# Where in SBUF the expert weights and the x operands begin: rests by 256 bytes in an attention and two-expert kernel

## Chip, cores and metric

The kernel runs on one core of a Trainium2 chip. The metric is the device time of one execution in microseconds, a median over runs. Lower is better.

## What is computed

Attention with talking heads (2 batches, 12 heads, 448 positions, head size 64), and then two feed-forward layers, called experts here, over 896 tokens of width 768 with 2048 hidden units. All is float32.

```python
scores = scale * np.matmul(q, k.transpose(0, 1, 3, 2))
scores = np.einsum('bhij,hg->bgij', scores, w_pre)
attn = np.exp(scores - np.max(scores, axis=-1, keepdims=True))
attn = attn / (np.sum(attn, axis=-1, keepdims=True) + 1e-09)
attn = np.einsum('bhij,hg->bgij', attn, w_post)
x = merge_heads(np.matmul(attn, v))          # 896 x 768
h = x @ w_in1;  g = h * np.clip(h + 3.0, 0.0, 6.0) / 6.0;  x = g @ w_out1
h = x @ w_in2;  g = np.maximum(h, 0.0) + alpha * np.minimum(h, 0.0)
return g @ w_out2
```

## The kernel before

The attention comes first, 90 steps of ten query rows over all heads, pipelined by hand with an order written out in the source: a step's loads, its mixing matmuls, its exponentials and its products with v are spread over several steps. The four expert layers follow: in1 (768 to 2048), out1 (2048 to 768), in2 and out2. The first pieces of in1 are computed between the last attention steps.

An expert's weights come from HBM as 64-bit numbers, in blocks of 128 partitions by 768 columns, 16 blocks a layer and 64 in all. Each block is converted on the chip by a chain of seven instructions: ScalarE (L346, L347), VectorE (L354, L355, L362), GpSimd (L369), which make `wb`, and then ScalarE copies `wb` to the rounded high part `whi` (L374) and GpSimd takes the difference as the low part `wlo` (L380). In the loop of `in_layer` and of `out_layer` a block's `wst` is loaded four blocks ahead, its `wb` is made two to three blocks ahead, and its `whi` and `wlo` two blocks ahead.

Each product of the experts is three matmuls in the type float32r, written out in `mm3` (L432 to L436): `whi` by the operand's high part, `whi` by its low part, `wlo` by its high part. The weights are the stationary operand (128 columns, loaded anew for every matmul), the operands move (448 columns). In in1 and in2 the moving operands are the x pairs `xh` and `xl`, in out1 and out2 the g pairs `gh` and `gl`. One block of weights has 36 such matmuls in every layer, a layer has 576, and the four have 2304. All of them stand on L434 in the profile.

The tiles lie in pools that grow from both ends of a partition's bytes: those with `side="right"` from the end downwards, the others from the start upwards, in the order in which they are opened. A tile takes a multiple of 32 bytes. An x, g or `t` tile is 448 x 4 = 1792 bytes (7 x 256), a `whi`, `wlo` or `wb` tile 768 x 4 = 3072 (12 x 256), a `wst` tile 6144 (24 x 256), so all tiles of one of these pools share the rest by 256 of the pool's end. The right side ends at byte 229,344, which is 224 by 256. The rests of the first bytes before the change, in bytes by 256:

| tiles | pool, side | rest before |
|---|---|---|
| weights `wst`, `wb`, `whi`, `wlo` (blocks 3 on; `whi` and `wlo` of all) | `w`, right | 224 |
| `xh`, `xl` (both batches), `t` | `x0`, `x1`, `tmp`, right | 224 |
| `gh`, `gl`, the first two of batch 0 | `g0`, right | 224 |
| `gh`, `gl`, the other 30 of 32 | `g1`, left | 0 |
| attention: `kT` of heads 0 to 5, of heads 6 to 11 | `kq`, right | 32, 224 |
| attention: `qT` | `kq`, right | 32, 96, 160 |
| attention: scores `S` of even tiles | `s_even`, right | 64 |

`const` holds `alpha_sb` (64 bytes), `three` (L82, 32 bytes taken) and `warm` (L83, 32 bytes taken) on the left, ahead of all other left pools. `three` is the bias of the first expert's activation (L454). `warm` is the target of one exponential at the start (L102), which has the table loaded.

The pools `w`, `x0` and `g0` are opened in `open_early` (L389 to L396), when the attention's `kq` and `s_even` have been closed; `x1` and `tmp` follow in `open_x1`.

Of the kernel before, what the change touches and what calls it, by code (L numbers as in the profile page):

```python
# [7 lines left out]
F32 = mybir.dt.float32  # L8
# [27 lines left out]
def kernel(  # L36
# [42 lines left out]

    const = ctx.enter_context(tc.tile_pool(name="const", bufs=1))  # L80
    alpha_sb = const.tile([128, KF], F32, name="alpha_sb")
    three = const.tile([128, 1], F32, name="three")  # L82
    warm = const.tile([128, 1], F32, name="warm")  # L83


    p_xt, p_late, p_odd, p_kq, p_even, p_ps, p_sc = (ExitStack() for _ in range(7))
# [1 line left out]
    def pool(stack, name, **kw):  # L88
        return stack.enter_context(tc.tile_pool(name=name, reuse_waits="tile", **kw))

    xtp = pool(p_xt, "xt", bufs=1)
    late = pool(p_late, "late", bufs=3)
    s_odd = pool(p_odd, "s_odd", bufs=1)
# [5 lines left out]
    with tc.manual_schedule():  # L99
# [289 lines left out]
        def open_early():  # L389
            p_even.close()  # L390
            p_kq.close()
            p_sc.close()
            P["ps2"] = pool(ctx, "ps2", bufs=2, space=PSUM, side="right")
            P["w"] = pool(ctx, "w", bufs=2, side="right")
            P["x0"] = pool(ctx, "x0", bufs=KD, side="right")
            P["g0"] = pool(ctx, "g0", bufs=NE, side="right")  # L396

# [143 lines left out]
        for i in range(NC):  # L541
            at(a, lambda i=i: load_w(i))
            for z, f in enumerate((conv_magnitude, conv_shift, conv_sign, conv_round)):
                at(a + 3 + z, lambda f=f, i=i: f(i))
            a += 7
        at(X, open_early)
        at(X + 1, lambda: nc.sync.dma_start(out=alpha_sb, in_=alpha.rearrange("(k p) -> p k", p=128)))
        for kk in range(KD):
# [209 lines left out]
```

## Time and profile before

| | |
|---|---|
| time, median of 3 runs | 721.94 us (721.37 to 722.91) |
| the profiled execution's own time | 722.08 us |
| span of the profile, first to last instruction | 720.3 us |
| mean granted TensorE clock | 0.995 of full speed |
| TensorE matmul busy | 704.3 us (98% of the span), 4164 instructions |
| VectorE, ScalarE, GpSimd busy | 58%, 52%, 47% |

By the times at which their matmuls start, the stages are: attention to about 254 us (with pieces of in1 from 219 us on), in1 to 363 us, out1 to 481 us, in2 to 598 us, out2 to 716.8 us, then the last copy and store.

A matmul's row in the profile shows 0.36 to 0.37 us, while the next one starts some 0.20 us later: matmuls are pipelined, so the distance from one start to the next, called the step here, and not the length of the row, is what a matmul costs.

### The profile page before, as it was taken

How to read it: one execution, taken by the hardware profiler on the slowest of the kernel's cores; microseconds unless marked ns; L12 is line 12 of the kernel's file. 1: busy time of each engine (PE TensorE's matmuls, PEld its weight loads, DVE VectorE, ACT ScalarE, POOL GpSimd, SP SyncE). 2: the span in 40 equal slices, each digit the busy share in tenths (PEclk: the TensorE clock that was granted, in tenths of full speed). 3: DMA queues.
4: the chain of work that ended last, by engine and by line, in shares of the span. 5: the costliest groups of instructions: out<-in, count | busy, mean ns of one | idle time of the engine just before them, and what ended most of it. 6: DMA issues, size and time to landing. Idle time of an engine off the chain costs nothing.

```text
span 720.3 us, 11169 instructions
## 1 busy us (share of the span) xinstructions
PE 704.3 (98%) x4164; PEld 609.4 (85%) x4164; DVE 414.3 (58%) x790; ACT 376.6 (52%) x704; POOL 335.1 (47%) x224
## 2 busy tenths in 40 slices
PE   5999999999999998999999999999999999999998
PEld 2678777877778987888889999999999999999997
DVE  5564585456667367777773454347777777344301
ACT  4686666577777455666554443344545444434300
POOL 6331175112235145656567755435555556654530
PEclk9899999999999999999999999999999999999999
DMA  5752564356444023232333433322232333325302
GB/s 157 227 170 100 180 178 122 102 173 199 154 89 131 2 72 104 90 129 89 95 125 132 137 121 101 125 88 87 88 128 92 122 99 131 132 92 182 111 1 76
DMA packets 31875, 85.21 MB, mean 118 GB/s; under 512 B 5966, under 2 KB 21966, under 8 KB 31822
## 3 DMA queue, kind: packets, MB, share of 16 engines
q1 hardware_dynamic: 31822, 84.50, 36.4%
q8 instruction: 33, 0.54, 0.3%
q14 instruction: 20, 0.16, 0.1%
HBM read 62.47 MB, written 2.75 MB: 91 GB/s over the span
## 4 chain that ended last, share of the span: by engine, by line
PE 79%; issue 9%; POOL 8%; DVE 2%; ACT 1%; DMA 0%; SPq 0%; POOLq 0%; ACTq 0%; DVEq 0%
PE p L434 51%; PE pt L242 10%; PE mx L222 9%; PE av L279 5%; PE sc L195 4%; POOL wb L369 4%; POOL wlo L380 2%; POOL kT L158 1%; DMA kst<-in_k_dram 0%; DVE nm L224 0%; DVE wb L354 0%; DVE wr L216 0%; ACT wb L346 0%; DVE xl L293 0%; ACT xh L292 0%
## 5 line engine op out<-in xcount | busy, mean ns | idle before, releaser
L380 POOL TENSOR_TENSOR wlo<-wb,whi 128x768 fp32r<-128x768 f32 x64 | 132.5, 2071 | 163.7 <-ACT whi L374 161.3
L369 POOL TENSOR_TENSOR wb<-wb,wst 128x768 int32<-128x768 int32 x64 | 130.5, 2039 | 69.9 <-DVE wb L362 36.5
L434 PE MATMUL p<-xh,wlo 128*128 128x448 f32 x384 | 141.5, 369 | 3.0 <-POOL wlo L380 2.5
L434 PE MATMUL p<-xh,whi 128*128 128x448 f32 x384 | 142.9, 372 | 0.0
L434 PE MATMUL p<-gh,wlo 128*128 128x448 f32 x384 | 141.2, 368 | 0.1
L434 PE MATMUL p<-gh,whi 128*128 128x448 f32 x384 | 141.0, 367 | 0.0
L434 PE MATMUL p<-gl,whi 128*128 128x448 f32 x384 | 141.0, 367 | 0.0
L434 PE MATMUL p<-xl,whi 128*128 128x448 f32 x384 | 140.4, 366 | 0.0
L354 DVE TENSOR_SCALAR wb<-wb 128x768 f32<-128x768 f32 x64 | 63.9, 999 | 97.5 <-ACT wb L346 97.5
L346 ACT ACTIVATE wb<-wst 128x768 f32<-128x768 f32 x64 | 58.3, 911 | 77.0 <-DMA wst<-in_w_out_dram 46.4
L242 PEld LDWEIGHTS pt<-wr,e 120*112 120x112 f32 x720 | 86.8, 176 | 7.6 <-issue 2.3
L232 ACT ACTIVATE e<-mx,nm 120x448 f32<-120x448 f32 (+1 forms) x90 | 57.1, 635 | 64.5 <-DVE sm L213 44.7
L242 PE MATMUL pt<-wr,e 120*112 120x120 f32 x720 | 88.5, 266 | 0.0
L222 PE MATMUL mx<-pull,wmix_pre 120*120 120x448 f32 x180 | 85.7, 559 | 2.3 <-DMA pull<-S 2.3
L434 PEld LDWEIGHTS p<-xh,wlo 128*128 128x128 f32 x384 | 72.1, 188 | 13.0 <-POOL wlo L380 7.5
L224 DVE TENSOR_REDUCE nm<-mx 120x1 f32<-120x448 f32 (+1 forms) x90 | 56.0, 622 | 46.7 <-PE mx L222 46.7
L434 PEld LDWEIGHTS p<-xh,whi 128*128 128x128 f32 x384 | 72.1, 188 | 7.3 <-issue 1.2
L434 PEld LDWEIGHTS p<-gh,wlo 128*128 128x128 f32 x384 | 72.2, 188 | 7.3 <-POOL wlo L380 0.8
L434 PEld LDWEIGHTS p<-xl,whi 128*128 128x128 f32 x384 | 72.2, 188 | 6.8 <-issue 1.1
L434 PEld LDWEIGHTS p<-gl,whi 128*128 128x128 f32 x384 | 72.2, 188 | 6.6
L434 PEld LDWEIGHTS p<-gh,whi 128*128 128x128 f32 x384 | 72.2, 188 | 6.4
L374 ACT CAST whi<-wb 128x768 fp32r<-128x768 f32 x64 | 53.2, 831 | 46.2 <-PE p L434 43.8
(52 smaller groups left out, 862.4 us busy)
## 6 DMA issues: line engine op xcount, KB each, us to landing
wst<-in_w_in_dram SPq DMA_DIRECT2D x32, 768.0 KB
wst<-in_w_out_dram SPq DMA_DIRECT2D x32, 768.0 KB
pull<-S SPq DMA_DIRECT2D x88, 210.0 KB
qst<-in_q_dram SPq DMA_DIRECT2D x20, 180.0 KB
kst<-in_k_dram SPq DMA_DIRECT2D x5, 672.0 KB
v<-in_v_dram SPq DMA_DIRECT2D x8, 336.0 KB
out_dram<-o SPq DMA_DIRECT2D x12, 224.0 KB
qst<-in_q_dram SPq DMA_DIRECT2D x8, 132.0 KB
```

The source lines that it names most:

```text
L195: nc.tensor.matmul(p[:n, :S], t[:, o, a:a + n], kT[h], start=(o == 0), stop=(o == 1))
L222: nc.tensor.matmul(m[:pn, :S], wpre[:pn, :pn], d[:pn], start=True, stop=True)
L224: nc.vector.tensor_reduce(nm[:pn], m[:pn, :S], axis=AX.X, op=ALU.max, negate=True)
L232: nc.scalar.activation(out=e[:pn], in_=m[:pn, :S], func=ACTF.Exp, bias=nm[:pn], accum_out=sm[:pn])
L242: nc.tensor.matmul(p[:, c * GP:(c + 1) * GP], e[:pn, c * JP:(c + 1) * JP], wr[:pn], start=True, stop=True,)
L279: nc.tensor.matmul(p[64 * o:64 * o + 64, a % 3, :n], v_t[T["b"], h // HC][:, h % HC, c, :], MT[ti][:, c, h, :n], start=(c == 0), stop=(c = ...
L346: nc.scalar.activation(t, s[:, :, 1].bitcast(F32), ACTF.Abs)
L354: nc.vector.tensor_scalar(t, t, W_MAX, W_MIN, ALU.min, ALU.max)
L369: nc.gpsimd.tensor_tensor(n, n, st_t.pop(i)[:, :, 0].bitcast(I32), ALU.add)
L374: nc.scalar.copy(hi, b_t[i])
L380: nc.gpsimd.tensor_tensor(lo, b_t.pop(i), w_t[i][0].bitcast(F32), ALU.subtract)
L434: nc.tensor.matmul(p, wt[a], xt[c], start=(first and z == 0), stop=(last and z == 2))
```

## The change

`three` leaves the left `const` pool for a new pool `edge`, the first on the right side, where it takes 32 bytes. `warm` grows from 1 to 16 columns, 64 bytes, so `const` keeps its 128 bytes and every left pool its place. All that lies on the right moves down by 32 bytes. Behind the `w` pool a tile `gap` of 192 bytes is opened that nothing writes or reads, so `x0`, `g0`, `x1` and `tmp` move down by 224 bytes in all. No other instruction is changed.

```diff
     alpha_sb = const.tile([128, KF], F32, name="alpha_sb")
-    three = const.tile([128, 1], F32, name="three")
-    warm = const.tile([128, 1], F32, name="warm")
+    warm = const.tile([128, 16], F32, name="warm")
...
+    edge = pool(ctx, "edge", bufs=1, side="right")
+    three = edge.tile([128, 1], F32, name="three")
     xtp = pool(p_xt, "xt", bufs=1)
...
             P["w"] = pool(ctx, "w", bufs=2, side="right")
+
+            pool(ctx, "gap", bufs=1, side="right").tile([128, 48], F32, name="gap")
             P["x0"] = pool(ctx, "x0", bufs=KD, side="right")
```

The rests by 256 after it: weights 192; x pairs, `t` and all g pairs 0; `kT` 0 and 192; `qT` 0, 64 and 128; even `S` 32; left tiles as before.

## Rows read from the trace of the kernel before

**Rows 1.** The page, part 1: busy us, share of the span and instructions of each engine.

```profile
PE 704.3 (98%) x4164; PEld 609.4 (85%) x4164; DVE 414.3 (58%) x790; ACT 376.6 (52%) x704; POOL 335.1 (47%) x224
```

**Rows 2.** The chain that ended last: start us, us, what.

```profile
331.70 1.61 issue
333.31 2.27 POOL wb L369
...
363.93 352.92 PE p L434 x1726
```

**Rows 3.** Windows: stretch, length, busy of PE, PEld, DVE, ACT, POOL (instructions), clock, DMA.

```profile
254.00:364.00 110.00, 106.92 (x510) 94.57 (x510) 82.88 (x102) 66.40 (x101) 63.17 (x29) 1.00 0.30 101
...
371.60:421.00 49.40, 49.40 (x247) 46.36 (x248) 23.32 (x29) 22.11 (x29) 35.12 (x17) 1.00 0.40 131
429.00:481.00 52.00, 52.00 (x253) 47.31 (x252) 21.14 (x26) 18.84 (x24) 26.70 (x14) 1.00 0.35 115
482.00:597.00 115.00, 115.00 (x569) 106.57 (x568) 86.74 (x141) 54.93 (x79) 61.25 (x30) 1.00 0.30 98
602.00:657.00 55.00, 55.00 (x268) 50.06 (x267) 22.86 (x26) 20.25 (x26) 31.47 (x17) 1.00 0.39 131
```

**Rows 4.** Timeline of TensorE around its last stall, and where g0 operands return.

```profile
371.18 0.37 PE L434 MATMUL p<-gl,whi 128*128 128x448 f32 x1
371.54 0.47 PE L434 MATMUL p<-gh,wlo 128*128 128x448 f32 x1
371.85 0.36 PE L434 MATMUL p<-gh,whi 128*128 128x448 f32 x1
...
421.25 0.36 PE L434 MATMUL p<-gl,whi 128*128 128x448 f32 x1
421.45 0.36 PE L434 MATMUL p<-gh,wlo 128*128 128x448 f32 x1
```

**Rows 5.** Timeline of TensorE in out1, the second half: first and last of 250 matmuls.

```profile
429.42 0.37 PE L434 MATMUL p<-gh,wlo 128*128 128x448 f32 x1
...
480.88 0.37 PE L434 MATMUL p<-gh,wlo 128*128 128x448 f32 x1
```

**Rows 6.** Timeline of TensorE: first matmul of in2, first and last of out2.

```profile
481.08 0.36 PE L434 MATMUL p<-xh,whi 128*128 128x448 f32 x1
...
597.82 0.36 PE L434 MATMUL p<-gh,whi 128*128 128x448 f32 x1
...
716.46 0.37 PE L434 MATMUL p<-gh,wlo 128*128 128x448 f32 x1
```

**Rows 7.** Timeline of TensorE in in1: first and last of 26 matmuls between two stalls.

```profile
311.65 0.37 PE L434 MATMUL p<-xl,whi 128*128 128x448 f32 x1
...
316.82 0.37 PE L434 MATMUL p<-xh,wlo 128*128 128x448 f32 x1
```

**Rows 8.** Timeline of GpSimd: `wlo` in in1 (first two), in out1, in in2.

```profile
330.92 2.44 POOL L380 TENSOR_TENSOR wlo<-wb,whi 128x768 fp32r<-128x768 f32 x1 [2.96 <-ACT whi L374]
...
338.54 2.44 POOL L380 TENSOR_TENSOR wlo<-wb,whi 128x768 fp32r<-128x768 f32 x1 [2.96 <-ACT whi L374]
...
444.84 1.84 POOL L380 TENSOR_TENSOR wlo<-wb,whi 128x768 fp32r<-128x768 f32 x1 [3.74 <-ACT whi L374]
...
502.29 1.89 POOL L380 TENSOR_TENSOR wlo<-wb,whi 128x768 fp32r<-128x768 f32 x1 [1.91 <-ACT whi L374]
```

**Rows 9.** Groups of instructions, forms apart: the attention's matmuls in float32r.

```profile
L195 PE MATMUL sc<-kT,qT 128*120 128x448 f32 x120 | 53.6, 533 | 1.6 <-POOL kT L152 0.9 <-ACT S L586 0.4 <-POOL qT L168 0.3
L195 PE MATMUL sc<-kT,qT 128*88 128x448 f32 x48 | 22.1, 541 | 0.0
```

**Rows 10.** Timelines at the two ends: `warm` on ScalarE, the last copy on VectorE.

```profile
2.02 0.20 ACT L102 ACTIVATE warm<-warm 128x1 f32<-128x1 f32 x1
...
716.87 0.62 DVE L677 COPY o<-p 128x448 f32<-128x448 f32 x1 [1.85 <-PE p L434]
```

## The prediction, made before the change was run

> **What bounds the kernel now.** I read the engines' busy time first: TensorE is busy for 98% of the span [rows 1], at the full granted clock of 2.4 GHz in all expert stretches (1.00 in [rows 3]). Busy is not the same as fast, so I next asked the chain that ended last where the end is set. Its last piece is one unbroken run of 1726 expert matmuls, 352.92 us from 363.93 on [rows 2]: nothing but TensorE's own rate decides out1, in2 and out2. Ahead of it the chain runs through GpSimd and "issue" pieces, not through matmuls [rows 2]; TensorE is idle there for 3.1 of 110 us [rows 3]. So two stretches have two different limits: the conversion of weights in in1, the matmul rate behind it.
>
> Then I read that rate, as the distance between starts. 448 columns at 2.4 GHz would take 448 / 2.4 = 186.7 ns. The run averages 352.92 / 1726 = 204.5 ns, and it isn't one rate with noise but a few exact levels:
> - 371.85 to 421.45: 248 steps of 200.0 ns [rows 4], moving operands at rest 0, weights at 224.
> - 429.42 to 480.88: 249 steps of 206.7 ns [rows 5], the same rests, 0 and 224.
> - in2, 481.08 to 597.82: 576 steps of 202.7 ns on average [rows 6], both rests 224.
> - out2, 597.82 to 716.46: 575 steps of 206.3 ns [rows 6], mostly 0 and 224.
> - a piece of in1, 311.65 to 316.82: 25 steps of 206.8 ns [rows 7], both rests 224.
>
> Other engines don't make these levels: they hold for 50 us and more while VectorE, ScalarE, GpSimd and the DMAs come and go [rows 3]. 200.0 and 206.7 ns are 480 and 496 cycles of 2.4 GHz, 16 apart. The same pair of rests shows both, so the rest alone doesn't set the level. What came before does too: the 200.0 stretch begins right behind a stall (371.18, 371.54, 371.85 in [rows 4]), and the slower one when, at 421.45, the matmuls return to the four g0 tiles, the only g tiles at rest 224; between 421.45 and 429.42 there are 39 steps of 204.4 ns on average [rows 4, 5], and when the g0 tiles are over, the level stays at 206.7. Out2 enters from in2's operands at 224, and is slow throughout.
>
> **The change part by part.** The edits that add or grow an instruction first. `warm` with 16 columns instead of 1 is 15 more columns in an instruction of 0.20 us at 2.02 us [rows 10], ahead of all other work of ScalarE, which then has to wait for the first scores: nothing. If nothing covered it, it would cost under 0.1 us, since even a copy of 448 columns takes 0.62 us [rows 10]. `three` is read from another address by the same instruction; the gap has no instruction. The queues, the loads and the waits keep their order; SP issues the same DMAs. Left tiles keep their addresses.
>
> The attention's float32r products are 168 matmuls [rows 9] with kT and qT moved by 32 bytes. I have no step for these new rests. Priced by the levels above, each can change by at most 6.7 ns, 1.1 us for 168 either way; they now fall all over those levels, so I take 0 and keep 0.5 us on each side.
>
> In in1 a block of weights takes 7.62 us: `wlo` starts at 330.92 and at 338.54 [rows 8]. TensorE needs 36 x 202.7 ns = 7.30 us for it, and waits for the rest. The loop goes `wlo` on GpSimd, `wb` on ScalarE, the conversion on VectorE, the activation's steps behind it, `whi` on ScalarE, `wlo` again; GpSimd sits idle for 2.96 us before each `wlo` until `whi` is there [rows 8], while no matmul is the releaser. A step of 200.0 or 206.7 ns makes TensorE's part 7.20 or 7.44 us, both under 7.62, so I take 0 there. The cover is gone only from 7.62 / 36 = 211.7 ns on.
>
> What is left are the steps from 371.85 to 716.46. Of the chain's 1726 matmuls 37 begin before 371.85 [rows 2, 4], so it is 1726 - 37 - 1 = 1688 steps in 344.61 us, 204.2 ns each, with no idle time of TensorE in any window [rows 3]. After the change every moving operand of this stretch has rest 0 and every weight 192, the same from end to end. The trace doesn't show 0 with 192. The bounds: if TensorE lost nothing between matmuls, 186.7 ns; above, one more stride of 16 cycles, 213.3 ns. The nearest rows are those with the moving operand at 0: 200.0 and 206.7 ns. I take 200.0, for two reasons. First, the one time that operands at 0 were entered from a stall, the level was 200.0 and held for 248 steps through six blocks of weights [rows 4]; what ended it was the return of tiles at 224, and after the change no such tile is left. Second, if the step is a fetch or a start held to a grid of 16 cycles (6.67 ns, in which float32 operands of 4 bytes a column pass 64 bytes), then 192 and 0 are both multiples of 64 and 224 is not, which speaks for fewer lost slots and not for more. The second is an argument, not a row.
>
> The sum: 1688 x 200.0 = 337.6 us against 344.61, so -7.0 us. By stage, that is about -1.9 in out1, 576 x 2.7 = -1.5 in in2, 575 x 6.3 = -3.6 in out2. What would be late next is the conversion. In out1 it has been seen to keep up at 200.0 ns: no idle time from 371.6 to 421 [rows 3]. In in2 GpSimd waits 1.91 us before a `wlo` [rows 8], so it isn't full; if in2's conversion nevertheless allowed only today's 7.30 us a block, 1.5 us of the gain would be lost. The end (716.87 on, [rows 10]) moves along.
>
> The profiled execution took 722.08 us, its span 720.3 and 1.78 around it. That is 0.14 us over the median of 721.94. 722.08 - 7.0 - 0.1 = 715.0 us against the median.
>
> A rule that speaks against all this: the page "SBUF — State Buffer" of the Trainium skill, section "Who interferes with whom", gives TensorE two independent read ports, one for the moving operand and one for the weight load, and says that TensorE never waits on anyone. By it the place of the weights against x costs nothing, and the sum would be 0: 722 us. The trace neither refutes it (equal rests, two levels) nor explains the levels.
>
> **The rivals.**
> - The level is handed on by what came before and the address has no part in it. For it: one pair of rests shows 200.0 and 206.7 [rows 4, 5], and rests of 224 and 224 show 202.7 and 206.8 [rows 6, 7]. Against it: each switch in the run coincides with a change of rest or with a stall. Stalls are as before, so the levels would come out mixed as today: 721.9, within 1.4. The rule of the Trainium skill's page above says the same.
> - 0 with 192 settles at or near in2's average of 202.7: 1688 x 202.7 = 342.1, -2.5 us, 719.4; with stages at different levels, 717 to 721.5.
> - Slower: the stretch locks to 206.7 ns at 371.85. Then nothing breaks the lock up to the end, as nothing has in 249 steps [rows 5], and all stages pay: 1688 x 206.7 = 348.9, +4.3 us, 726.2. It is decided in the first few steps after the last stall. For it: it is the level held longest today. Against it: it has followed operands at 224 wherever I see it begin. One stride further, 213.3 ns, would make in1 wait for TensorE too: +15.5 and some 1 us, about 738.
> - A level not seen yet, below 200: one stride of 16 cycles down is 193.3 ns, 1688 x 193.3 = 326.3, -18.3 us, 703.6. Against it: both rests of g have been tried, and no run of steps under 200 stands in the trace. The change would have to act through the weights' rest alone.
> - That the rests aren't what the change says would need a left tile or a closing pool to move; `const` keeps 64 + 64 = 128 bytes, so I give it nothing of its own.
>
> **How the numbers follow.** Locked to 200.0, 715.0 us (714 to 716.5): 0.42. Near 202.7 or mixed stages: 0.20, of it 0.14 faster by over 0.2% (1.4 us, about what a measurement of this kernel can tell from no change) and 0.06 not. Address without effect: 0.08. Locked to 206.7: 0.18. Below 200: 0.08. Above 207: 0.04. Faster 0.42 + 0.14 + 0.08 = 0.64, same 0.06 + 0.08 = 0.14, slower 0.18 + 0.04 = 0.22. The range leaves out the two unseen levels and the outer edges: from 713.5 (714.0 less the attention's 0.5) to 726.5 (726.2 and some of the same).
>
> **What would show it.** Starts 200.0 ns apart from the last stall of in1 or out1 to 709 us, 7.20 us from block to block in out1, in2 and out2 alike, and no jump at the two returns of the g0 tiles. In1's blocks should stay at 7.62 us, with TensorE idle longer in each. I am wrong if the steps are 206.7 throughout, if the level still changes in mid-stage with all rests equal, or if in2 stops at 7.30 us with TensorE waiting for `wlo`.

## The result, and the profile after

The changed kernel takes 714.6 us (median of 4 executions, 713.94 to 715.41), against 721.66 us of the kernel before, run again beside it. The ratio is 0.9894, with a 95% interval of 0.9882 to 0.9906: 1.1% faster. The profiled execution took 715.01 us, 7.07 us less than that of before (722.08), and its span is 713.2 us.

The chain that ended last (start us, us, what) still ends in one run of expert matmuls on TensorE, now counted from the last stall:

```profile
371.52 338.30 PE p L438 x1690
```

338.30 / 1690 = 200.2 ns a matmul; the first step behind the stall is longer, 0.31 us (371.52 to 371.83 below). The line numbers are four higher, the matmul is the same. TensorE's timeline shows the last stall, the place where the g0 tiles used to raise the step, the first matmul of in2, and the first and last of out2:

```profile
371.02 0.37 PE L438 MATMUL p<-gl,whi 128*128 128x448 f32 x1
371.52 0.47 PE L438 MATMUL p<-gh,wlo 128*128 128x448 f32 x1
371.83 0.37 PE L438 MATMUL p<-gh,whi 128*128 128x448 f32 x1
...
421.04 0.36 PE L438 MATMUL p<-gh,whi 128*128 128x448 f32 x1
421.23 0.36 PE L438 MATMUL p<-gl,whi 128*128 128x448 f32 x1
421.44 0.36 PE L438 MATMUL p<-gh,wlo 128*128 128x448 f32 x1
421.64 0.36 PE L438 MATMUL p<-gh,whi 128*128 128x448 f32 x1
...
479.24 0.36 PE L438 MATMUL p<-xh,whi 128*128 128x448 f32 x1
...
594.43 0.36 PE L438 MATMUL p<-gh,whi 128*128 128x448 f32 x1
...
709.43 0.37 PE L438 MATMUL p<-gh,wlo 128*128 128x448 f32 x1
```

From 371.83 to 709.43 there are again 1688 steps, in 337.60 us: 200.0 ns each, where the kernel before had 204.2 [rows 4, 6]. In2 is 576 steps in 115.19 us (116.74 before, [rows 6]), out2 575 in 115.00 (118.64 before). There is no jump at 421.45 any more [rows 4]. One detail is new: the 200.0 is an average over three. Starts lie 0.19, 0.21 and 0.20 us apart in turn (421.04 to 421.64), where the 200.0 of before had equal steps.

In1 has kept its pace. The windows and GpSimd's timeline:

```profile
254.00:364.00 110.00, 106.46 (x511) 95.98 (x510) 82.86 (x102) 66.47 (x102) 63.04 (x29) 0.98 0.30 101
371.60:421.00 49.40, 49.40 (x247) 46.31 (x248) 23.00 (x29) 22.10 (x29) 34.81 (x17) 1.00 0.40 132
429.00:479.00 50.00, 50.00 (x251) 46.87 (x251) 22.40 (x26) 18.64 (x24) 25.83 (x14) 1.00 0.36 117
480.00:594.00 114.00, 114.00 (x571) 106.85 (x571) 87.24 (x141) 55.48 (x79) 61.25 (x31) 1.00 0.31 100
```

```profile
330.95 2.43 POOL L382 TENSOR_TENSOR wlo<-wb,whi 128x768 fp32r<-128x768 f32 x1 [2.96 <-ACT whi L376]
...
338.57 2.43 POOL L382 TENSOR_TENSOR wlo<-wb,whi 128x768 fp32r<-128x768 f32 x1 [2.96 <-ACT whi L376]
...
500.20 1.89 POOL L382 TENSOR_TENSOR wlo<-wb,whi 128x768 fp32r<-128x768 f32 x1 [1.88 <-ACT whi L376]
...
507.40 1.89 POOL L382 TENSOR_TENSOR wlo<-wb,whi 128x768 fp32r<-128x768 f32 x1 [1.88 <-ACT whi L376]
```

A block of in1 takes 7.62 us as before [rows 8], and TensorE is idle a little longer in it (3.5 of 110 us, 3.1 before [rows 3]). In in2 the conversion follows TensorE at 7.20 us a block (500.20, 507.40), and TensorE has no idle time in the windows shown from 371.6 on.

### The profile page after: what moved, and what is told of

It is laid out like the page before. It is cut to its first block, busy times and chain, and to the rows that moved or that the text cites. A ratio compares the mean times of both kernels' runs of the same rounds, so it can differ in the third digit from the quotient of the medians.

```text
span 713.2 us, 11169 instructions
## 1 busy us (share of the span) xinstructions
PE 695.8 (98%) x4164; PEld 609.3 (85%) x4164; DVE 415.1 (58%) x790; ACT 376.1 (53%) x704; POOL 334.7 (47%) x224
## 4 chain that ended last, share of the span: by engine, by line
PE 77%; issue 9%; POOL 6%; DVE 2%; DMA 2%; ACT 1%; SPq 1%; POOLq 0%; ACTq 0%; DVEq 0%
PE p L438 49%; PE pt L244 9%; PE mx L224 9%; PE av L281 5%; POOL wb L371 4%; PE sc L197 4%; POOL wlo L382 2%; DMA pull<-S 2%; DMA kst<-in_k_dram 1%; DVE nm L226 0%; ACT S L525 0%; DVE wb L356 0%; SPq L127 0%; DVE wr L218 0%; ACT wb L348 0%
## 5 line engine op out<-in xcount | busy, mean ns | idle before, releaser
L438 PE MATMUL p<-gh,wlo 128*128 128x448 f32 x384 | 139.6, 363 | 0.3
L438 PE MATMUL p<-gl,whi 128*128 128x448 f32 x384 | 139.2, 362 | 0.0
L438 PE MATMUL p<-gh,whi 128*128 128x448 f32 x384 | 138.3, 360 | 0.0
L197 PE MATMUL sc<-kT,qT 128*120 128x448 f32 (+1 forms) x168 | 75.1, 533 | 1.2 <-POOL kT L154 0.9
```

The source lines that it names most:

```text
L197: nc.tensor.matmul(p[:n, :S], t[:, o, a:a + n], kT[h], start=(o == 0), stop=(o == 1))
L438: nc.tensor.matmul(p, wt[a], xt[c], start=(first and z == 0), stop=(last and z == 2))
```

## What was tried, and what it showed

Two arguments of the prediction made different demands on other placements. Four theories stand in the expectations: A, both rests have to be multiples of 64 (the prediction's second reason); B, only the difference, weights' rest less operand's rest by 256, counts (new); C, the address has no part, and the level is handed on from the last stall (the prediction's first rival); and later D, which joins B with the entry: the difference sets which levels there are, and the entry behind a stall chooses where there are two. In the expectations of whole kernels C stands in a weaker form, nearer to the prediction's first reason: operands of one rest throughout are enough for 200.0.

In all whole kernels but the changed one itself the constant stays on the left, and the pads stand in `open_early` or later, so the attention's tiles lie as before the change. Their diffs are against the kernel before.

### The step alone, for all pairs of rests

A kernel of its own; the part that matters, shortened:

```diff
+        def burst(n, wr, xr, reps):
+            p = ps.tile([128, 512], F32, tag="p", name="p")[:, :448]
+            for i in range(reps * 12):
+                k = i % 6 * 128
+                for z, (u, v) in enumerate(((0, 0), (0, 448), (768, 0))):
+                    nc.tensor.matmul(p, w[wr][:, u + k:u + k + 128], x[xr][:, v:v + 448], ...)
+            nc.scalar.copy(os[n % 12], p)
...
+        for xr in range(0, 256, 32):
+            for wr in range(0, 256, 32):
+                burst(n, wr, xr, 1)
...
+        for wr in range(224, -1, -32):
+            for xr in range(224, -1, -32):
+                burst(n, wr, xr, 1)
```

> Measures the disputed step by itself. The kernel leaves out the whole computation of the reference: it runs 128 bursts of 36 float32r matmuls (448 columns, the same order of high and low parts as L434), each burst behind a stall, over all 64 pairs of a weight rest and an x rest by 256 (0, 32, ... 224), every pair twice, in different orders. Theory A (what counts is that both rests are multiples of 64): 200.0 ns per step for the 16 pairs of multiples of 64, and higher levels, 202 to 207 ns, for the other 48, with pairs that show two levels. Theory B (what counts is the difference of the two rests): the 64 pairs fall into 8 classes by difference, the same step within a class, 200.0 ns for weights 192 bytes ahead of x. Theory C (the address has no part, only what came before): no order by rests; the two bursts of one pair differ as much as two pairs.

The tiles are named by rest, a for 0, b for 32, to h for 224. TensorE's timeline, merged by burst (start us, us from the first start to the last end, the names, the count, idle time before it), for the operands at rest 192 (`xg`), first pass and a part of the second:

```profile
411.55 7.55 PE L53 MATMUL p<-xg,wa 128*128 128x448 f32 x36 [0.68 <-ACT o L57]
419.77 7.69 PE L53 MATMUL p<-xg,wb 128*128 128x448 f32 x36 [0.68 <-ACT o L57]
428.14 7.61 PE L53 MATMUL p<-xg,wc 128*128 128x448 f32 x36 [0.68 <-ACT o L57]
436.44 7.66 PE L53 MATMUL p<-xg,wd 128*128 128x448 f32 x36 [0.68 <-ACT o L57]
444.77 7.48 PE L53 MATMUL p<-xg,we 128*128 128x448 f32 x36 [0.68 <-ACT o L57]
452.93 7.70 PE L53 MATMUL p<-xg,wf 128*128 128x448 f32 x36 [0.68 <-ACT o L57]
461.31 7.57 PE L53 MATMUL p<-xg,wg 128*128 128x448 f32 x36 [0.68 <-ACT o L57]
469.56 7.58 PE L53 MATMUL p<-xg,wh 128*128 128x448 f32 x36 [0.68 <-ACT o L57]
...
683.88 7.48 PE L53 MATMUL p<-xg,wf 128*128 128x448 f32 x36 [0.68 <-ACT o L57]
749.89 7.47 PE L53 MATMUL p<-xg,we 128*128 128x448 f32 x36 [0.68 <-ACT o L57]
...
947.30 7.48 PE L53 MATMUL p<-xg,wb 128*128 128x448 f32 x36 [0.68 <-ACT o L57]
```

A burst of 7.48 us has steps of 200.0 ns; 0.22 us more over 34 steps are 6.5 ns more (`wf`, 7.70). `we` has the weights at 128, and 128 - 192 is 192 by 256: 7.48 and 7.47 in the two passes. `wf` (a difference of 224) and `wb` (96) take 7.70 and 7.69 in one pass and 7.48 in the other. Taken from the starts of the 6th and the 36th matmul, the 128 bursts give this, by the difference:

| weights less operand, by 256 | step, ns (16 bursts each) |
|---|---|
| 0 | 202.7 in 15 |
| 32 | 203.3 in 7, 204.4 to 204.5 in 8 |
| 64 | 202.2 in 16 |
| 96 | 200.0 in 13, 206.7 in 3 |
| 128 | 204.0 in 16 |
| 160 | 205.3 in 16 |
| 192 | 200.0 in 16 |
| 224 | 200.0 in 8, 204.5 in 1, 206.6 to 206.7 in 7 |

(The first two bursts of the program, one each at 0 and 32, are left out: the first starts with steps of 0.37 us, and from 20 to 26 us, in which the second starts, the granted clock is 0.50 of full speed, that is 1.2 GHz.) The order is by difference: at 0, 64, 128, 160 and 192 all pairs of a difference give the same step, whether their rests are multiples of 64 or not. Theory A falls: weights at 64 with operands at 0 are 202.2, weights at 224 with operands at 32 are 200.0. Theory C falls too. B holds, but not as it was put: at 32, 96 and 224 the same difference has more than one level, in some pairs from one burst to the other. At 96 all three bursts at 206.7 belong to two of the eight pairs (weights at 0 with operands at 160, both times; 32 with 192, once), so a part of the pair itself isn't excluded there.

### One side at a time, in the whole kernel

```diff
# x0_w224
+            pool(ctx, "gap", bufs=1, side="right").tile([128, 56], F32, name="gap")
             P["x0"] = pool(ctx, "x0", bufs=KD, side="right")
# all192
+            pool(ctx, "edge", bufs=1, side="right").tile([128, 8], F32, name="edge")
             P["w"] = pool(ctx, "w", bufs=2, side="right")
# x224_w192
+            pool(ctx, "edge", bufs=1, side="right").tile([128, 8], F32, name="edge")
             P["w"] = pool(ctx, "w", bufs=2, side="right")
+            pool(ctx, "gap", bufs=1, side="right").tile([128, 56], F32, name="gap")
```

> x pairs, t and g0 at rest 0 as in the change, weights stay at 224, the attention's tiles stay where they were before the change. Theory A: the weights at 224 aren't a multiple of 64, so the steps of out1, in2 and out2 stand at 200.0 or 206.7 ns, by the entry behind the last stall: 714.6 us if it locks low, 726 if it locks high, and runs that differ from each other. Theory B: a difference of 224, which has shown both 200.0 and 206.7: no statement between these. Theory C (uniform operands are enough, the lock follows the stall): 200.0 throughout, 714.6 us, the same as the change.

> Weights, x pairs, t and g0 at rest 192, the other g tiles at 0, the attention's tiles as before the change. Theory A: all multiples of 64, so 200.0 ns everywhere from the last stall on, 714.6 us. Theory B: in in1 and in2 the difference is 0 as in the kernel before, so in2 stays at 202.7 ns and only out1 and most of out2 come to 200.0: 716 us. Theory C: operands of two rests alternate in out1 and out2, so the lock can be lost at the g0 tiles as before: mixed levels, 718 to 722 us.

> Weights at rest 192 as in the change, x pairs, t and g0 at 224, the other g tiles at 0, the attention's tiles as before the change. Theory A: in2's x operands aren't multiples of 64, so in2 stays above 200 (202 to 207 ns, 116.5 to 119 us for the stage), while out1 and out2 are at 200.0 except around the g0 tiles: 716 to 719 us. Theory B: a difference of 224 in in2, 192 in most of out1 and out2: those at 200.0, in2 at 200.0 or 206.7. Theory C: mixed levels as before, 718 to 722 us. If the weights' rest alone makes the level, 714.6 us.

Measured: 714.66 us (ratio 0.9904, 0.9888 to 0.9921), 716.19 us (0.9924, 0.9909 to 0.9938) and 719.19 us (0.9961, 0.9946 to 0.9976). TensorE's timeline of `all192`, first matmul of in2, first and last of out2:

```profile
478.65 0.36 PE L435 MATMUL p<-xh,whi 128*128 128x448 f32 x1
...
595.39 0.36 PE L435 MATMUL p<-gh,whi 128*128 128x448 f32 x1
...
710.55 0.37 PE L435 MATMUL p<-gh,wlo 128*128 128x448 f32 x1
```

In2 takes 116.74 us, 202.7 ns a step, as in the kernel before, though all its rests are now multiples of 64: the difference is still 0. Out2 takes 115.16 us, 200.3 ns. TensorE's timeline of `x224_w192` at the two ends of in2:

```profile
479.35 0.37 PE L436 MATMUL p<-xh,whi 128*128 128x448 f32 x1
...
598.39 0.37 PE L436 MATMUL p<-gh,whi 128*128 128x448 f32 x1
```

119.04 us, 206.7 ns a step, the upper level of a difference of 224. The g0 tiles at a difference of 224 among others at 192 cost out1 and out2 next to nothing. So 719.19 is 714.6 and 3.8 more in in2 (119.04 less the 115.2 of 200.0 ns), with 0.8 us left over. B's statements for `all192` and `x224_w192` are met, and for `x0_w224` it made none between the levels. A's in2 of `all192` at 200.0 failed, and its range for `x224_w192` (716 to 719) was missed by 0.2 us. C's 714.6 for `x0_w224` came out in these four executions, its 718 to 722 for `all192` failed, and for `x224_w192` the time lies in its range, but not the way it had it: in2 alone pays, and the other stages aren't mixed.

### Rests that are no multiples of 64, and a placement that should be slow

The `lead` of `x32_w224` stands in `open_late`.

```diff
# x32_w224
+            pool(ctx, "gap", bufs=1, side="right").tile([128, 48], F32, name="gap")
             P["x0"] = pool(ctx, "x0", bufs=KD, side="right")
...
+            pool(ctx, "lead", bufs=1).tile([128, 8], F32, name="lead")
             P["g1"] = pool(ctx, "g1", bufs=2 * KF - NE)
# x0_w160
+            pool(ctx, "edge", bufs=1, side="right").tile([128, 16], F32, name="edge")
             P["w"] = pool(ctx, "w", bufs=2, side="right")
+            pool(ctx, "gap", bufs=1, side="right").tile([128, 40], F32, name="gap")
# x0_w96
+            pool(ctx, "edge", bufs=1, side="right").tile([128, 32], F32, name="edge")
             P["w"] = pool(ctx, "w", bufs=2, side="right")
+            pool(ctx, "gap", bufs=1, side="right").tile([128, 24], F32, name="gap")
```

> All x and g pairs at rest 32, all weights at 224: no rest is a multiple of 64, the difference is 192 as in the change; the attention's tiles as before the change. Theory B: 200.0 ns from the last stall on in out1, in2 and out2, 714.6 us. Theory A (multiples of 64): 202 to 207 ns, 718 to 726 us.

> All x and g pairs at rest 0, weights at 160; the attention's tiles as before the change. Theory B: a difference of 160 gave 205.3 ns in the table, all twelve and more bursts alike: 1688 x (205.3 - 204.2) = +1.9 us, 723.9 us, slower than the kernel before, 7.39 us per block of weights. Theory C (uniform operands are enough): 200.0 ns, 714.6 us.

> All x and g pairs at rest 0, weights at 96; the attention's tiles as before the change. Theory B: a difference of 96 gave 200.0 ns in all bursts of the table: 714.6 us, the same as the change. Theory A (multiples of 64): above 200 ns, 718 us or more.

`x32_w224`: 715.14 us (0.9907, 0.989 to 0.9924), the change's gain with no rest at a multiple of 64. Its in2, from its first matmul to the first of out2, is 115.20 us, 200.0 ns a step:

```profile
478.87 0.36 PE L436 MATMUL p<-xh,whi 128*128 128x448 f32 x1
...
594.07 0.36 PE L436 MATMUL p<-gh,whi 128*128 128x448 f32 x1
```

`x0_w160`: 724.07 us (1.003, 1.0018 to 1.0042), slower than the kernel before, 0.2 us from what the table's 205.3 ns gave. Its in2 is 118.27 us, 205.3 ns a step:

```profile
482.01 0.37 PE L436 MATMUL p<-xh,whi 128*128 128x448 f32 x1
...
600.28 0.37 PE L436 MATMUL p<-gh,whi 128*128 128x448 f32 x1
```

`x0_w96`: 714.47, 713.88 and 715.44 us in three executions, and 725.63 in a fourth, so its expectation of 714.6 us failed in one of four. It had named the table wrongly: that has 206.7 ns in three bursts of sixteen at 96.

### Do the levels change from one execution to the next?

The three kernels are the changed one, `x0_w224` and `x0_w96`, unaltered, with more executions. A profile is of one execution.

> The changed kernel itself, more executions. In the table of steps a difference of 192 showed 200.0 ns in all 16 bursts. Theory D (the difference sets which levels there are, and the entry behind a stall chooses among them; 192 has only one): all executions within 713.9 to 715.5 us. If 192 has a second level of 206.7 ns too: some executions near 726.

> x and g pairs at 0, weights at 224, more executions. In the table a difference of 224 showed 200.0 ns in 8 of 16 bursts and 204.5 to 206.7 in the others. Theory D: in a share of the executions the last stall leads to 206.7 ns, 714.6 + 1688 x 6.7 ns = 725.9 us, or to 206.7 up to some stage; the rest at 714.6. If the entry is the same in each execution: all at 714.6.

> x and g pairs at 0, weights at 96, more executions. The table has 200.0 ns in 13 of 16 bursts at a difference of 96 and 206.7 in 3 (not in all, as was written for the run before this), and one execution of four took 725.63 us. Theory D: most at 714.6 us and some at 725.7 to 725.9, none between. If 725.63 was an outside disturbance: all at 714.6.

The change: 714.42 to 715.4 us in 4 executions, beside 713.94 to 715.41 before. `x0_w224`: ten executions from 714.59 to 716.74 us, two at 722.59 and 724.2. `x0_w96`: four from 714.5 to 716.03 us, three from 725.98 to 727.41. The profiles of `x0_w224` and `x0_w96` are of long executions, at a granted clock of 0.997 and 0.998 of full speed, so the upper levels can be seen at work in the whole kernel. TensorE's timeline of `x0_w224` at 722.59 us, first matmul of in2, first of out2:

```profile
481.69 0.36 PE L435 MATMUL p<-xh,whi 128*128 128x448 f32 x1
...
599.45 0.36 PE L435 MATMUL p<-gh,whi 128*128 128x448 f32 x1
```

117.76 us, 204.4 ns a step: the level that the table has once at 224 (204.5), not the 206.7 expected. 1688 x 4.4 ns = 7.4 us, 722.0. The execution of 724.2 us has no profile. TensorE's timeline of `x0_w96` at 727.41 us, the same two matmuls:

```profile
483.96 0.37 PE L436 MATMUL p<-xh,whi 128*128 128x448 f32 x1
...
603.00 0.37 PE L436 MATMUL p<-gh,whi 128*128 128x448 f32 x1
```

119.04 us, 206.7 ns a step. D holds: where a difference has two levels the same program comes out at either, and both profiled executions kept theirs from the last stall to the end. In1, where TensorE stalls once in each block, shows the choice inside one execution. Three stretches between stalls of the profiled `x0_w224`, 30 steps from the first line to the second of each:

```profile
334.57 0.36 PE L435 MATMUL p<-xl,whi 128*128 128x448 f32 x1
...
340.57 0.37 PE L435 MATMUL p<-xl,whi 128*128 128x448 f32 x1
...
342.20 0.37 PE L435 MATMUL p<-xl,whi 128*128 128x448 f32 x1
...
348.40 0.37 PE L435 MATMUL p<-xl,whi 128*128 128x448 f32 x1
...
349.82 0.37 PE L435 MATMUL p<-xl,whi 128*128 128x448 f32 x1
...
355.95 0.37 PE L435 MATMUL p<-xl,whi 128*128 128x448 f32 x1
```

200.0, 206.7 and 204.3 ns, with the same tiles' rests. A difference of 0 has a second level too, which the table's 15 bursts missed: [rows 7] are a stretch at 206.8 ns with equal rests between others at 202.7, and in the in1 of `all192`, with the difference 0 as well, four stretches are at 206.7. A difference of 192 has come out at one level everywhere: by their times in all 8 executions of the change and in 4 each of `x32_w224` and of the next kernel, and by the steps in every stretch between stalls from 254 us on of their four profiles (12 of 35 matmuls and more in each, 199.9 to 200.1 ns).

### The attention's part

```diff
+            pool(ctx, "edge", bufs=1, side="right").tile([128, 8], F32, name="edge")
             P["w"] = pool(ctx, "w", bufs=2, side="right")
+            pool(ctx, "gap", bufs=1, side="right").tile([128, 48], F32, name="gap")
```

> One part of the change alone: the constant's place is kept, a pad of 32 bytes is opened ahead of the weights' pool in open_early, and the gap of 192 follows. The experts' rests are those of the change (weights 192, x and g 0); the attention's tiles (kT, qT, S) lie as before the change. The prediction's reading (the attention's new rests are worth 0, at most 0.5 us either way): 714.6 us. If the attention's new rests give or take a part of the 7 us: over 0.5 us away from the change.

714.73 us (0.9897, 0.9884 to 0.9909), beside 714.81 of the change in the same comparison. The 32 bytes by which the attention's tiles move are worth nothing that can be measured.

### Is there a placement under 200 ns?

The diff is against the kernel of the table, shortened:

```diff
-    x = {32 * z: place(32 * z, f"x{c}", 2 * 448) for z, c in enumerate(LETTERS)}
-    w = {32 * z: place(32 * z, f"w{c}", 2 * 768) for z, c in enumerate(LETTERS)}
+    x = place(0, "x", 1024)
+    w = place(0, "w", 1664)
...
+        for j in range(64):
+            burst(n, j, 0)
...
+        for j in range(63, -1, -1):
+            burst(n, 0, j)
```

> Leaves out the whole computation of the reference. The same bursts of 36 matmuls as in the table, with differences in steps of 4 bytes: 64 bursts with x at rest 0 and the weights at 0, 4, ... 252, then 64 with the weights at 0 and x at 252, 248, ... 0. Theory B (only the difference weights less x by 256 counts): the second half repeats the first at the same differences; at multiples of 32 it gives the levels of the table (0: 202.7, 32: 203 to 204.5, 64: 202.2, 96: 200.0, 128: 204.0, 160: 205.3, 192: 200.0, 224: 200.0 or 204.5 to 206.7 ns). Theory A' (lines of 16 bytes matter besides): starts that aren't multiples of 16 bytes are slower than their neighbours. If some difference gives under 200.0 ns, a faster placement exists; if 200.0 is the floor, none.

The first 64 bursts move the weights by 4 bytes each, the others the operands. No burst of the 128 is under 200.0 ns, and they go up to 215.6 (the first one, 248.2, which starts with steps of 0.37 us, left out). At the multiples of 32 the levels of the table come back (202.7, 204.4, 202.2, 200.0, 204.0, 205.3, 200.0 in the second half, and 206.7 at 224). Between them the halves mostly disagree: at a difference of 48 it is 202.2 with the weights off and 204.0 with the operands off, at 80 it is 203.3 and 204.2, at 208 204.4 and 203.0. So the rule of the difference is shown for starts at multiples of 32 bytes and no finer; whether off that grid it fails or the entry chooses, one burst each doesn't tell. A' fails as well: with the weights off, 108 and 140 are at 200.0, under 112 (204.0) and 144 (204.4) beside them. 200.0 ns is the floor of what was tried; a placement that beats the change wasn't found.

## Why the prediction was right, point by point

**The bound.** Right. The stretch from 371.85 on was TensorE's step and nothing else, and the 1688 steps gave -7.01 us (344.61 to 337.60) where the sum had -7.0. By stage: out1 from 371.85 on -1.82 (about -1.9 forecast), in2 -1.55 (-1.5), out2 -3.64 (-3.6).

**In1 and the attention at nothing.** Right. In1 stayed at 7.62 us a block, and out1 begins at 363.20 us (363.31 before). The table's levels, all under 207 ns, never reach the 211.7 ns at which TensorE would have set in1's pace. The attention's part is within 0.1 us by `x0_w192_late`.

**The step of 200.0.** The value was right, by luck as far as its two reasons go: one was wrong and the other incomplete. "192 and 0 are both multiples of 64 and 224 is not" was no row, and it is refuted: `x32_w224` is as fast without a multiple of 64, and in2 of `all192` is at 202.7 with nothing else. That 0 entered from a stall had been at 200.0 was a true row [rows 4], but of a difference of 224, which comes out at 200.0 or above from one execution to the next: `x0_w224` has every operand at 0 behind the last stall too, and one of its executions stands at 204.4 to the end. What makes the change's 200.0 safe is that a difference of 192 has had one level in every try. The rows of before could not show it, since no expert matmul there had a difference other than 0 or 224: in the kernel before in2 had 0 and stood at 202.7 [rows 6], in1 had 0 and stood at 202.7 or, in one stretch, 206.8 [rows 7], and the g operands at rest 0 had 224 and took 200.0 and 206.7 [rows 4, 5].

**The rivals.** "The address has no part" is refuted by `x0_w160`, which differs from `x0_w192_late` by the weights' place alone and is 9.3 us longer (724.07 and 714.73). Its other half, that a level is handed on by what came before, is right where a difference has two levels. The page "SBUF — State Buffer" of the Trainium skill says in "Who interferes with whom" that TensorE has two independent read ports, one for the moving operand and one for the weight load, and never waits on anyone. What the prediction drew from it, that the place of the weights against x costs nothing, doesn't hold here: placements differ by up to 6.7 ns a matmul. Whether the two ports get in each other's way no run shows. "Locked to 206.7" was a real case, and near the price named (726.2 us): `x0_w96` shows it at 725.63 and at 725.98 to 727.41. What stood against it, that 206.7 had followed operands at 224, was no rule: in `x0_w96` it begins with all operands at 0. It has been seen at the differences 0, 96 and 224, not at 192. "Under 200" found nothing in its favour.

**The signs named in advance.** Steps of 200.0 to 709 us, 7.20 us from block to block in in2, no jump at the g0 tiles, in1 at 7.62: all seen. That the 200.0 is made of three unequal steps was not foreseen; in the table, too, all 16 bursts at 192 have them, while those at 200.0 at 96 and 224 have equal steps.

**What stays open.** Why the difference counts. Weight loads and matmuls overlap in the profile (busy 609.4 and 704.3 of 720.3 us, [rows 1]), so a dependence on where the one reads against the other is plausible; but no run separates the load from the matmul, and this is argued, not shown. Nor is it known what in the entry chooses between two levels.

## What to carry to other kernels

Where a chain of float32r matmuls sets the time, read the distance between starts and not the length of the rows: a few exact levels that change at stalls or at other tiles speak of placement. For matmuls of this shape (128 weight columns loaded for each, 448 moving columns), place the weights 192 bytes ahead of the moving operands, by 256, for all operand tiles of the chain; equal rests cost 1.3% of each step here or more, and differences of 96 and 224 are as fast only in some executions. Before believing a rule for a placement from one trace, sweep the pair of addresses in bursts behind stalls, and take each more than once.

## What the runs showed that was not expected

- A table of steps by difference with a period of 256 bytes, which doesn't follow alignment: 96 and 192 have 200.0 ns, while 0, 64 and 128 have 202.7, 202.2 and 204.0.
- One program can have executions 11 us and more apart (`x0_w96`, 714.5 and 725.98 us and more). In its two profiles (714.47 and 727.41 us) the 1688 steps behind the last stall at 200.0 and 206.7 ns make 11.3 of the 12.9 us.
- In the profile of the change TensorE's granted clock fell in in1, behind an idle time of 1.80 us. TensorE's timeline at its end, and windows of 4 us (busy time of PE, PEld, DVE, ACT, POOL, then the granted clock):

```profile
280.14 0.47 PE L438 MATMUL p<-xh,wlo 128*128 128x448 f32 x1 [1.80 <-POOL wlo L382]
...
278.00:282.00 4.00, 2.20 (x9) 1.67 (x7) 2.86 (x4) 2.60 (x5) 4.00 (x2) 0.85 0.00 0
282.00:286.00 4.00, 4.00 (x16) 3.63 (x15) 3.32 (x6) 2.19 (x4) 1.04 (x2) 0.72 0.56 197
286.00:290.00 4.00, 4.00 (x22) 3.75 (x21) 2.86 (x3) 2.80 (x4) 3.92 (x2) 1.00 0.00 0
```

The clock stood at 0.72 of full speed on average over 4 us, which means a part of it at 1.2 GHz. In1, which waits for the conversion, didn't get longer by it: out1 begins at 363.20 us (363.31 before).
